# Summing Up's seven products inside PSUM, with ScalarE copying running sums, in a GFNet plus MLP-Mixer kernel

## The chip, the cores and the metric

One core of one Trainium2 chip. The metric is device time in microseconds of one execution; lower is better. A core has TensorE (matrix products into PSUM banks), VectorE and ScalarE (element-wise work, both read PSUM), GpSimd and SyncE (here mostly DMA issue and some sums).

## The reference

All fp32; batch 8, sequence 3008, width 256.

```python
X = np.fft.rfft(x, axis=1)                    # x: (8, 3008, 256)
y = np.fft.irfft(X * (filt_r + 1j * filt_i), n=3008, axis=1)
h = np.maximum(y.transpose(0, 2, 1) @ w_tok1, 0) @ w_tok2     # 3008 -> 256 -> 3008
u = y + h.transpose(0, 2, 1)
out = u + np.maximum(u @ w_ch1, 0) @ w_ch2    # 256 -> 1536 -> 256
```

## The kernel before

The transforms are products with DFT tables in two factors (47 x 64). A first stretch transforms batch 0 and rounds and combines the fp32 weights. From there the loop `mix` runs: for 8 batches, 6 tiles of the sequence (`m`, 512 columns, the last 448), 6 blocks of the hidden width (`jp`), one iteration each, 288 in all. Beside them the generator `dft` works off the next batch's transform in pieces; `mix` yields at marked places of an iteration (0, 1, 1.5, 2) and the outer loop decides there whether a piece is emitted. Instructions of an engine stand in the order in which this Python emits them (`manual_schedule`); nothing reorders them.

Both channel products, Up (256 to 1536, then ReLU) and Down (1536 to 256), are done block by block with a seven-product scheme (Strassen-Winograd) on 2x2 blocks. A product is one `matmul` call of 128x128 weights with 256 columns (224 in the last tile), and the chip executes it as two passes, each with its own weight load.

For Up, the right-hand sums `v` (4 x 256 columns) are made once a tile by `u_sums`, and the sums over the seven products give the four blocks of `hh`: `up_first` (L977) computes products 0, 5, 6 and 4 into the four halves of two PSUM banks (`pg`, two buffers), and ScalarE copies product 0 to SBUF (L980, tile `s`). `up_middle` has VectorE add product 5 to it, and then that to products 6 and 4. `up_last` (L993) computes products 1, 2 and 3 into banks that have been read, VectorE makes the four blocks by two sums of 512 columns, and ScalarE applies the ReLU to each pair of blocks (L998). All VectorE sums go through `v`, so they show as L955.

Down lags by one iteration. `h_sums` make the four sums `t` of the previous iteration's `hh` on VectorE (one of 512 columns, two of 256), and `down` (L1011) multiplies `hh` and `t` into four banks `po`, which accumulate over the six `jp`. When a tile's last block has passed, `finish` adds the banks to `u`: ScalarE copies one part (L1071), VectorE does the rest in steps (`a`, `b_`, `c`, `d`, two transposes), taken from a list two at a time by `one_step`; two of them right at the end of the iteration. The output leaves through GpSimd's queue (L1019).

The next tile's `u` is computed by `u_part` at fixed places (`own`, `new`); its products stand at L898. The token product of the next batch (L841, ended by VectorE's `c` sums and ScalarE's L858) stands in each batch's 33rd iteration. The transform's spectral products are VectorE's L709, two of 1024 columns, followed by L714 and L715; their results are copied by ScalarE (L692). ScalarE's other transform copies are L544.

One iteration emits, in this order: `up_first` and `up_middle`; `h_sums`; Down part 0 (three products); a part of the next `u`; a place for transform work; `up_last`; steps of `finish`; Down part 1 (two products); a place; Down part 2 (two products); `finish` when a tile is complete; a place.

Of the kernel before, what the change touches and what calls it, by code (L numbers as in the profile page):

```python
# [10 lines left out]
FP32 = mybir.dt.float32  # L11
I64 = mybir.dt.int64
U32 = mybir.dt.uint32
AF = mybir.ActivationFunctionType
# [9 lines left out]
P = 128  # L24
# [104 lines left out]
def kernel(  # L129
# [11 lines left out]
    nc = tc.nc  # L141
# [34 lines left out]
    tp = pool("tp", 2)  # L176
    vp = pool("vp", 2)
    sp = pool("sp", 1)
# [4 lines left out]
    def bank(tag):  # L183
        return (psg if tag == "pg" else psum).tile([P, 512], FP32, tag=tag, name="ps_" + tag)
# [30 lines left out]
    chan = []  # L215
# [653 lines left out]
    def width(m):  # L869
        return 512 if m < MT - 1 else 448  # L870
# [83 lines left out]
    def v(out, in0, in1, op=ALU.add):  # L954
        nc.vector.tensor_tensor(out=out, in0=in0, in1=in1, op=op)  # L955
# [12 lines left out]
    def h_sums(hh, t, w):  # L968

        h = hh[:, :, 0:w // 2]  # L970
        return sums(t[:, :, 0:w // 2], h[:, 1:3], h[:, 0:2], h[:, 0], h[:, 3])

    def up_first(jp, ut, vt, w, g):
        hw = w // 2
        for ps, n, mov in ((g[0][:, 0], 0, ut[:, 0, 0:hw]), (g[0][:, 1], 5, vt[:, 2, 0:hw]),
                           (g[1][:, 0], 6, vt[:, 0, 0:hw]), (g[1][:, 1], 4, vt[:, 1, 0:hw])):
            nc.tensor.matmul(ps[:, 0:hw], chan[0][:, jp, n, :], mov, start=True, stop=True)  # L977

        s = sp.tile([P, 3, 256], FP32, tag="s", name="s")[:, :, 0:hw]
        nc.scalar.copy(out=s[:, 0], in_=g[0][:, 0, 0:hw])  # L980
        return s

    def up_middle(hh, w, g, s):
        hw = w // 2
        u2 = hh[:, 2, 0:hw]
        v(u2, g[0][:, 1, 0:hw], s[:, 0])
        v(s[:, 1:3], g[1][:, :, 0:hw], u2.unsqueeze(1).to_broadcast([P, 2, hw]))

    def up_last(jp, ut, vt, w, g, s, hh):
        hw = w // 2  # L990
        for ps, n, mov in ((g[0][:, 0], 1, ut[:, 1, 0:hw]), (g[0][:, 1], 2, ut[:, 1, hw:w]),
                           (g[1][:, 1], 3, vt[:, 3, 0:hw])):
            nc.tensor.matmul(ps[:, 0:hw], chan[0][:, jp, n, :], mov, start=True, stop=True)  # L993
        h = hh[:, :, 0:hw]
        for i, add in enumerate((s[:, 0:2], s[:, 2].unsqueeze(1).to_broadcast([P, 2, hw]))):
            hs = h[:, 2 * i:2 * i + 2]
            v(hs, g[i][:, :, 0:hw], add)
            nc.scalar.activation(out=hs, in_=hs, func=AF.Relu)  # L998

    def down(m, jp, part, hh, t, po):  # L1000
        hw = width(m) // 2
        if not po:
            for i in range(4):
                po.append(bank("po%d" % i).rearrange("p (s n) -> p s n", s=2))
        b11, b21, b22 = (hh[:, i, 0:hw] for i in (0, 3, 2))
        t1, t3, t2, t4_ = (t[:, i, 0:hw] for i in range(4))

        todo = (((0, 0, 1, 0, 1, b21), (0, 1, 0, 1, 2, b22), (2, 0, 1, 0, 0, b11)),
                ((1, 1, 1, 0, 6, t1), (3, 0, 1, 1, 4, t3)), ((2, 1, 0, 1, 5, t2), (1, 0, 0, 1, 3, t4_)))
        for i, j, first, last, n, mov in todo[part]:  # L1010
            nc.tensor.matmul(po[i][:, j, 0:hw], chan[1][:, jp, n, :], mov, start=(jp == 0 and first == 1),  # L1011
                             stop=(jp == JP - 1 and last == 1))
# [89 lines left out]
    h1s, uts, vts = {}, {}, {}  # L1102
# [22 lines left out]
    def mix(next_ready):  # L1125

        wait = []
        pos, hhs, tts = {}, {}, {}

        def loads(b):  # L1130
            if b + 1 < B and next_ready(b):
                for c in wait:
                    t4_load(b + 1, c)
                wait.clear()


        own = ({(3, 0): (0,), (3, 2): (1,)}, {(2, 2): (0,), (3, 0): (1,), (3, 2): (2, 3)})
        new = {(JP - 2, 0): (0, 1), (JP - 1, 0): (2, 3)}

        def u_parts(b, m, jp, place):  # L1140
            parts = own[b > 0] if m + 1 < MT else new if b + 1 < B else {}
            now = parts.get((jp, place), ())
            b, m = (b, m + 1) if m + 1 < MT else (b + 1, 0)
            for part in now:
                u_part(b, m, part)
            if now and now[-1] == max(p for ps in parts.values() for p in ps):
                if m:
                    wait.append(m)
                todo_v.extend(v_steps(b, m))
                if b and (b, m) < (B - 1, MT - 2):  # L1150
                    w2m_load((m + 2) % MT)

        to_dram = [f for m in range(MT) for f in w2_sums(m)]
        w1_todo, w1_out = w1_sums()
        items = [(b, m, jp) for b in range(B) for m in range(MT) for jp in range(JP)]
        n = MT * JP
        for i in range(len(items) + 1):
            now, old = i < len(items), i >= 1
            if not now:
                bo, mo, jo = items[i - 1]  # L1160
                t = tp.tile([P, 4, 256], FP32, tag="t", name="t")
                last_item(bo, mo, jo, hhs.pop(i - 1), t, uts[bo, mo], pos[bo, mo])
                break
            if JP - 2 <= i < JP + 2:
                for _ in range(6 if i > JP - 2 else 1):
                    if w1_todo:
                        w1_todo.pop(0)()
            elif i >= 2 * JP and i % 2 and w1_out:
                w1_out.pop(0)()
            if i and ended[0] < len(tiles):  # L1170
                convert_middle()
                convert_end(False)
                convert_middle()
            if now:
                b, m, jp = items[i]
                if i % n == 0:
                    wait.append(0)
                w = width(m)
                hhs[i] = hp.tile([P, 4, 256], FP32, tag="hh", name="hh")
                g = [bank("pg").rearrange("p (s n) -> p s n", s=2) for _ in range(2)]  # L1180
                s = up_first(jp, uts[b, m], vts[b, m], w, g)
                up_middle(hhs[i], w, g, s)
            while todo_h1:
                todo_h1.pop()()
            if i < JP:
                one_step()
            if old:
                bo, mo, jo = items[i - 1]
                tts[i - 1] = tp.tile([P, 4, 256], FP32, tag="t", name="t")
                for f in h_sums(hhs[i - 1], tts[i - 1], width(mo)):  # L1190
                    f()
                down(mo, jo, 0, hhs[i - 1], tts[i - 1], pos.setdefault((bo, mo), []))
            if now:
                u_parts(b, m, jp, 0)
            copies()
            yield b, i % n, 0
            if ended[0] < len(tiles):
                if i == 0:
                    convert_middle()
                convert_end(False)  # L1200
            if now:
                up_last(jp, uts[b, m], vts[b, m], w, g, s, hhs[i])
                if b + 1 < B and i % n == n - 4:
                    t4_sums(b + 1, 0)
            one_step()
            if i >= JP:
                one_step()
            if now and b + 1 < B:
                if n - 4 - W1S <= i % n < n - 4:
                    w1_load(i % n - (n - 4 - W1S))  # L1210
                if i % n == n - 4:
                    t4_sums(b + 1, 1)
            copies()
            loads(b)
            yield b, i % n, 1
            if old:
                down(mo, jo, 1, hhs[i - 1], tts[i - 1], pos[bo, mo])
            yield b, i % n, 1.5
            if old:
                down(mo, jo, 2, hhs.pop(i - 1), tts.pop(i - 1), pos[bo, mo])  # L1220
                if jo == JP - 1:
                    todo_v.extend(finish(bo, mo, uts[bo, mo], pos[bo, mo]))
                    one_step()
                    one_step()
            if now:
                if b + 1 < B and i % n == n - 4:
                    h1s[b + 1] = yield from token_product(b + 1)
                u_parts(b, m, jp, 2)
                if jp == JP - 1:
                    while todo_v and m + 1 == MT:  # L1230
                        one_step()
                if i >= 8 and to_dram:
                    to_dram.pop(0)()
                if i in (28, 29):
                    w2m_load(i - 28)
            loads(b)
            yield b, i % n, 2
        while todo_v:
            one_step()

    with tc.manual_schedule():
# [69 lines left out]
        n = MT * JP  # L1311
# [58 lines left out]
```

## Time and profile before

| | |
|---|---|
| time, median of 3 runs (lowest to highest) | 2405.31 us (2405.25 to 2406.09) |
| span of the profiled execution | 2403.2 us |
| what lies around the span, against the median | 2.1 us |
| TensorE busy | 2359.4 us, 98% |
| VectorE busy | 1951.0 us, 81% |
| ScalarE busy | 689.8 us, 29% |
| GpSimd busy | 638.3 us, 27% |
| granted TensorE clock, mean | 0.995 |
| the mixing loop begins | at about 140 us |

The profiled execution has no time of its own beside its span; the runs were timed without a profile. In the profile PE is a matmul pass on TensorE, PEld its weight load, DVE VectorE, ACT ScalarE, POOL GpSimd. Matmul passes overlap, so that a PE that is busy throughout can still have a little room; where it matters, the distance from one pass's start to the next tells more than the busy share.

### The profile page before, as it was taken

The numbers are of one execution on the slowest core, as the hardware profiler recorded it, in microseconds if no ns is written. First come the engines' busy times: TensorE is split into PE (matmuls) and PEld (weight loads), VectorE is DVE, ScalarE is ACT, GpSimd is POOL, SyncE is SP. The second block draws the span as 40 slices with busy tenths as digits, with TensorE's granted clock in tenths as the row PEclk, the third lists the DMA queues.
The fourth block names the chain that finished last, engine by engine and source line by source line (L and its number), as shares of the span: only waits on it lengthen the run. The fifth ranks groups of instructions, "written<-read, shape, count | busy, mean of one in ns | idle before, by whom it ended". The sixth has DMA issues, their size and how long they took to land.

```text
span 2403.2 us, 37053 instructions
## 1 busy us (share of the span) xinstructions
PE 2359.4 (98%) x13132; PEld 2012.9 (84%) x13132; DVE 1951.0 (81%) x3669; ACT 689.8 (29%) x1339; POOL 638.3 (27%) x1124
## 2 busy tenths in 40 slices
PE   7989999999999999999999999999999999999998
PEld 4667888888898888988888888988889888898887
DVE  7798887788887888788887788778887788877786
ACT  5732222222223222232222222222222322212222
POOL 7477434211211121112112311221121112112121
PEclk8999999999999999999999999999999999999999
DMA  9963546333353333533344333533335433331100
GB/s 218 241 195 121 152 119 226 114 118 85 106 188 124 100 95 117 189 118 96 98 145 158 117 93 103 186 120 107 90 114 172 132 98 98 108 130 32 39 14 21
DMA packets 189719, 294.28 MB, mean 122 GB/s; under 512 B 34444, under 2 KB 124962, under 8 KB 189534
## 3 DMA queue, kind: packets, MB, share of 16 engines
q1 hardware_dynamic: 148046, 231.24, 31.0%
q0 software_dynamic: 34688, 53.83, 8.6%
q10 hardware_dynamic: 6800, 6.85, 0.9%
q8 instruction: 104, 1.70, 0.3%
q14 instruction: 81, 0.66, 0.1%
HBM read 209.06 MB, written 82.72 MB: 121 GB/s over the span
## 4 chain that ended last, share of the span: by engine, by line
PE 92%; DVE 3%; DMA 2%; issue 1%; POOL 1%; ACT 1%; SPq 0%; ACTq 0%; DVEq 0%; POOLq 0%
PE ps_po L1011 35%; PE ps_pg L977 20%; PE ps_pg L993 15%; PE ps_b L528 3%; PE ps_b L841 3%; PE ps_acc L898 3%; PE ps_acc L841 2%; PE ps_pg L528 2%; PE ps_b L898 2%; PE ps_b L876 2%; PE ps_acc L876 2%; DVE both L284 0%; DVE t L955 0%; DMA g_tmp<-t 0%; DVE both L289 0%
## 5 line engine op out<-in xcount | busy, mean ns | idle before, releaser
L1019 POOL DMA_DIRECT2D out_dram<-r x752 | 408.3, 550 | 1452.0 <-issue 1028.0
L998 ACT ACTIVATE hh<-hh 128x512 f32<-128x512 f32 (+1 forms) x576 | 348.0, 621 | 1017.7 <-DVE hh L955 1013.8
L955 DVE TENSOR_TENSOR hh<-ps_pg,s 128x512 f32<-128x512 f32 (+3 forms) x864 | 482.5, 586 | 171.3 <-ACT s L980 161.1
L1011 PE MATMUL ps_po<-t,wc 128*128 128x256 f32 (+1 forms) x2296 | 558.1, 380 | 0.7 <-DVE t L955 0.7
L1011 PEld LDWEIGHTS ps_po<-t,wc 128*128 128x128 f32 x2296 | 427.7, 190 | 95.6 <-issue 38.7
L977 PE MATMUL ps_pg<-v,wc 128*128 128x256 f32 (+1 forms) x1728 | 412.6, 375 | 1.4 <-POOL wc L386 1.4
L1011 PE MATMUL ps_po<-hh,wc 128*128 128x256 f32 (+1 forms) x1722 | 411.5, 375 | 0.6 <-POOL wc L387 0.6
L977 PEld LDWEIGHTS ps_pg<-v,wc 128*128 128x128 f32 x1728 | 327.9, 190 | 39.6 <-POOL wc L386 2.2
L1011 PEld LDWEIGHTS ps_po<-hh,wc 128*128 128x128 f32 x1722 | 326.8, 190 | 38.4 <-POOL wc L387 1.4
L993 PE MATMUL ps_pg<-u,wc 128*128 128x256 f32 (+1 forms) x1152 | 292.3, 376 | 5.7 <-DVE hh L955 5.6
L955 DVE TENSOR_TENSOR t<-t,hh 128x256 f32<-128x256 f32 (+1 forms) x576 | 247.1, 429 | 19.8
L993 PEld LDWEIGHTS ps_pg<-u,wc 128*128 128x128 f32 x1152 | 217.2, 190 | 37.1 <-DVE hh L955 10.8
L955 DVE TENSOR_TENSOR s<-ps_pg,hh 128x512 f32<-128x512 f32 (+1 forms) x288 | 196.1, 681 | 30.0
L980 ACT COPY s<-ps_pg 128x256 f32<-128x256 f32 (+1 forms) x288 | 105.8, 368 | 332.4 <-PE ps_pg L977 329.1
L955 DVE TENSOR_TENSOR t<-hh 128x512 f32<-128x512 f32 (+1 forms) x288 | 194.4, 675 | 0.6 <-ACT hh L998 0.6
L977 PE MATMUL ps_pg<-u,wc 128*128 128x256 f32 (+1 forms) x576 | 169.3, 376 | 3.9 <-DVE hh L955 3.9
L993 PE MATMUL ps_pg<-v,wc 128*128 128x256 f32 (+1 forms) x576 | 169.2, 375 | 0.0
L977 PEld LDWEIGHTS ps_pg<-u,wc 128*128 128x128 f32 x576 | 108.1, 190 | 19.7 <-DVE hh L955 7.5
L993 PEld LDWEIGHTS ps_pg<-v,wc 128*128 128x128 f32 x576 | 109.2, 190 | 13.0
L955 DVE TENSOR_TENSOR u<-ps_acc,u 128x256 f32<-128x256 f32 (+1 forms) x84 | 46.2, 550 | 72.4 <-PE ps_acc L898 50.1
L955 DVE TENSOR_TENSOR u<-ps_b,u 128x512 f32<-128x512 f32 (+2 forms) x126 | 74.5, 591 | 28.8 <-PE ps_b L898 26.7
L898 PE MATMUL ps_acc<-w 128*128 128x256 f32 (+1 forms) x336 | 85.2, 376 | 0.0
(164 smaller groups left out, 2686.8 us busy)
## 6 DMA issues: line engine op xcount, KB each, us to landing
w<-w_tmp SPq DMA_DIRECT2D x84, 448.0 KB
w<-w_tmp SPq DMA_DIRECT2D x35, 896.0 KB
out_dram<-r POOLq DMA_DIRECT2D x696, 32.0 KB, 3.4
g_tmp<-t SPq DMA_DIRECT2D x112, 192.0 KB
t<-g_tmp SPq DMA_DIRECT2D x42, 512.0 KB
t<-z_tmp SPq DMA_DIRECT2D x196, 96.0 KB
z_tmp<-t SPq DMA_DIRECT2D x72, 256.0 KB
wb<-wbi_t SPq DMA_DIRECT2D x56, 256.0 KB
```

The lines of the kernel that those rows point to most:

```text
L528: nc.tensor.matmul(outs(i, j), stat(i, j), mov(i, j), start=True, stop=True)
L841: nc.tensor.matmul(ps[:, at], w[:, n], mov, start=(j == 0 and i in (0, 2)), stop=(j == AP - 1 and i >= 5))
L876: nc.tensor.matmul(ps[:, ds(q * P, n)], t4[b, c][:, r, ts(dh, P)], wai[:, 0:n], start=(first and q == 0), stop=(not first and q == 3))
L898: nc.tensor.matmul(ps[:, ds(j * hw, hw)], h1[:, n, :], w2m[m % 2][:, at, 0:hw], start=(i < 2 and j == 0), stop=(j == len(todo) - 1))
L955: nc.vector.tensor_tensor(out=out, in0=in0, in1=in1, op=op)
L977: nc.tensor.matmul(ps[:, 0:hw], chan[0][:, jp, n, :], mov, start=True, stop=True)
L980: nc.scalar.copy(out=s[:, 0], in_=g[0][:, 0, 0:hw])
L993: nc.tensor.matmul(ps[:, 0:hw], chan[0][:, jp, n, :], mov, start=True, stop=True)
L998: nc.scalar.activation(out=hs, in_=hs, func=AF.Relu)
L1011: nc.tensor.matmul(po[i][:, j, 0:hw], chan[1][:, jp, n, :], mov, start=(jp == 0 and first == 1), stop=(jp == JP - 1 and last == 1))
L1019: q.dma_start(bass.AP(tensor=ob.tensor, offset=ob.offset + row * D + g * cw, ap=[[N1 * D, 32], [D if h else -D, n], [1, cw]]), blocks[ts(g ...
```

## The change

Up's sums move into the accumulation of the banks. In one bank a half, `x`, takes products 0, 5, 6 and 2 one on top of the other, and ScalarE copies the running sum out after each (into `hh` blocks 0, 3 and 2; the last one goes through the ReLU straight into block 1). In the other bank, half `z` holds product 1, and half `y` product 4 and later 3 on top of it. VectorE adds `z` to block 0, the earlier `y` to block 2 and the later `y` to block 3, and ScalarE applies the ReLU to each block on its own. `h_sums` of the previous iteration come ahead of Up's sums, and Down is cut into four parts that stand between Up's steps.

```diff
-    def up_first(jp, ut, vt, w, g):
...
-        for ps, n, mov in ((g[0][:, 0], 0, ut[:, 0, 0:hw]), (g[0][:, 1], 5, vt[:, 2, 0:hw]),
-                           (g[1][:, 0], 6, vt[:, 0, 0:hw]), (g[1][:, 1], 4, vt[:, 1, 0:hw])):
-            nc.tensor.matmul(ps[:, 0:hw], chan[0][:, jp, n, :], mov, start=True, stop=True)
-
-        s = sp.tile([P, 3, 256], FP32, tag="s", name="s")[:, :, 0:hw]
-        nc.scalar.copy(out=s[:, 0], in_=g[0][:, 0, 0:hw])
-        return s
-
-    def up_middle(hh, w, g, s):
...
-    def up_last(jp, ut, vt, w, g, s, hh):
...
+    def up_steps(jp, ut, vt, w, hh):
+        hw = w // 2
+        one, two = (bank("pg").rearrange("p (s n) -> p s n", s=2)[:, :, 0:hw] for _ in range(2))
         h = hh[:, :, 0:hw]
+
+        def times(out, n, mov, start=False):
+            nc.tensor.matmul(out, chan[0][:, jp, n, :], mov, start=start, stop=True, skip_group_check=True)
+
+        def joined(i, ps):
+            v(h[:, i], ps, h[:, i])
+            nc.scalar.activation(out=h[:, i], in_=h[:, i], func=AF.Relu)
+
+        x, y, z = one[:, 0], two[:, 0], two[:, 1]
+        times(x, 0, ut[:, 0, 0:hw], start=True)
+        nc.scalar.copy(out=h[:, 0], in_=x)
+        times(z, 1, ut[:, 1, 0:hw], start=True)
+        times(y, 4, vt[:, 1, 0:hw])
+        times(x, 5, vt[:, 2, 0:hw])
+        nc.scalar.copy(out=h[:, 3], in_=x)
+        joined(0, z)
+        yield
+        times(x, 6, vt[:, 0, 0:hw])
+        nc.scalar.copy(out=h[:, 2], in_=x)
+        joined(2, y)
+        yield
+        times(x, 2, ut[:, 1, hw:w])
+        nc.scalar.activation(out=h[:, 1], in_=x, func=AF.Relu)
+        times(y, 3, vt[:, 3, 0:hw])
+        joined(3, y)
+        yield
...
-        todo = (((0, 0, 1, 0, 1, b21), (0, 1, 0, 1, 2, b22), (2, 0, 1, 0, 0, b11)),
-                ((1, 1, 1, 0, 6, t1), (3, 0, 1, 1, 4, t3)), ((2, 1, 0, 1, 5, t2), (1, 0, 0, 1, 3, t4_)))
+        todo = (((2, 0, 1, 0, 0, b11), (0, 1, 1, 0, 2, b22)), ((0, 0, 0, 1, 1, b21), (1, 1, 1, 0, 6, t1)),
+                ((3, 0, 1, 1, 4, t3),), ((2, 1, 0, 1, 5, t2), (1, 0, 0, 1, 3, t4_)))
...
-                g = [bank("pg").rearrange("p (s n) -> p s n", s=2) for _ in range(2)]
-                s = up_first(jp, uts[b, m], vts[b, m], w, g)
-                up_middle(hhs[i], w, g, s)
+                ups = up_steps(jp, uts[b, m], vts[b, m], w, hhs[i])
+            if old:
+                bo, mo, jo = items[i - 1]
+                tts[i - 1] = tp.tile([P, 4, 256], FP32, tag="t", name="t")
+                for f in h_sums(hhs[i - 1], tts[i - 1], width(mo)):
+                    f()
+            if now:
+                next(ups)
             while todo_h1:
                 todo_h1.pop()()
             if i < JP:
                 one_step()
             if old:
-                bo, mo, jo = items[i - 1]
-                tts[i - 1] = tp.tile([P, 4, 256], FP32, tag="t", name="t")
-                for f in h_sums(hhs[i - 1], tts[i - 1], width(mo)):
-                    f()
                 down(mo, jo, 0, hhs[i - 1], tts[i - 1], pos.setdefault((bo, mo), []))
+            if now:
+                next(ups)
+            if old:
+                down(mo, jo, 1, hhs[i - 1], tts[i - 1], pos[bo, mo])
             if now:
                 u_parts(b, m, jp, 0)
             copies()
...
             if now:
-                up_last(jp, uts[b, m], vts[b, m], w, g, s, hhs[i])
+                next(ups)
...
             yield b, i % n, 1
             if old:
-                down(mo, jo, 1, hhs[i - 1], tts[i - 1], pos[bo, mo])
+                down(mo, jo, 2, hhs[i - 1], tts[i - 1], pos[bo, mo])
             yield b, i % n, 1.5
             if old:
-                down(mo, jo, 2, hhs.pop(i - 1), tts.pop(i - 1), pos[bo, mo])
+                down(mo, jo, 3, hhs.pop(i - 1), tts.pop(i - 1), pos[bo, mo])
```

More of the change, by code (lines that the diff above doesn't have):

```diff
@@ L983, in up_middle @@
-    def up_middle(hh, w, g, s):
[L984 to L987, printed above, removed]
-    def up_last(jp, ut, vt, w, g, s, hh):
[L990 to L993, printed above, removed]
-        h = hh[:, :, 0:hw]
[L995 to L998, printed above, removed]
+        one, two = (bank("pg").rearrange("p (s n) -> p s n", s=2)[:, :, 0:hw] for _ in range(2))
```

## The prediction

> **What bounds the kernel now.** I read the page first, then stretches, waits, groups by form, and last the timeline of single iterations of the mixing loop. Page and a 200 us stretch:
>
> ```profile
> PE 2359.4 (98%) x13132; PEld 2012.9 (84%) x13132; DVE 1951.0 (81%) x3669; ACT 689.8 (29%) x1339; POOL 638.3 (27%) x1124
> ...
> PE 92%; DVE 3%; DMA 2%; issue 1%; POOL 1%; ACT 1%; SPq 0%; ACTq 0%; DVEq 0%; POOLq 0%
> ```
>
> ```profile
> 1100.00:1300.00 200.00, 200.00 (x1208) 175.80 (x1210) 166.18 (x317) 51.50 (x104) 37.84 (x69) 1.00 0.42 127
> ```
>
> PE is never idle there, at clock 1.00, and owns 92% of the ending chain. VectorE's 81% is off the path: relieving it buys nothing unless PE waits for it. The waits say how little PE does:
>
> ```profile
> PE ps_pg L993 <- DVE hh L955: 5.6, 4, 3.2
> PE ps_pg L977 <- DVE hh L955: 3.9, 4, 2.1
> ```
>
> The prices, by form (busy, mean ns):
>
> ```profile
> L998 ACT ACTIVATE hh<-hh 128x512 f32<-128x512 f32 x480 | 294.8, 630 | 861.0 <-DVE hh L955 857.1 <-DMA z_tmp<-t 3.9
> L955 DVE TENSOR_TENSOR hh<-ps_pg,s 128x256 f32<-128x256 f32 x240 | 101.4, 422 | 137.9 <-ACT s L980 137.8
> L980 ACT COPY s<-ps_pg 128x256 f32<-128x256 f32 x240 | 89.3, 372 | 304.7 <-PE ps_pg L977 301.5 <-DMA z_tmp<-t 1.9 <-ACT t L544 1.2
> ```
>
> Timeline of an iteration after a tile's end, and of the next one's start (start, length):
>
> ```profile
> 1203.10 0.59 PE L977 MATMUL ps_pg<-u,wc 128*128 128x256 f32 x2
> 1203.53 1.46 PE L977 MATMUL ps_pg<-v,wc 128*128 128x256 f32 x6
> 1204.22 0.37 ACT L980 COPY s<-ps_pg 128x256 f32<-128x256 f32 x1 [0.78 <-PE ps_pg L977]
> 1204.75 0.41 DVE L955 TENSOR_TENSOR r<-ps_po,r 128x256 f32<-128x256 f32 x1
> 1205.60 0.69 DVE L955 TENSOR_TENSOR s<-ps_pg,hh 128x512 f32<-128x512 f32 x1
> 1206.21 0.68 DVE L955 TENSOR_TENSOR t<-hh 128x512 f32<-128x512 f32 x1
> 1206.92 0.89 DVE L955 TENSOR_TENSOR t<-t,hh 128x256 f32<-128x256 f32 x2
> ...
> 1211.23 0.59 PE L977 MATMUL ps_pg<-u,wc 128*128 128x256 f32 x2
> ...
> 1211.57 1.21 DVE L709 TENSOR_TENSOR p<-ps_acc,filt 128x1024 f32<-128x1024 f32 x1
> ```
>
> A product is two matmul passes. Six take 1.46 us, one lasts 0.38, so a pass starts every 0.216 and a product every 0.432. From an iteration's first pass, the last operation of `finish` queued ahead ends at 1204.75+0.41-1203.10 = 2.06; the spectral product (L709) ends at 1.55. Today that is harmless.
>
> **What goes and comes.** Per iteration VectorE loses one 256-column sum (0.42) and three 512-column ones (0.69), 2.49 us, for three of 256, 1.27 us: 1.2 us x 288 = 350 us off VectorE, all off the path. `h_sums` move ahead of Up's sums on VectorE, three instructions without a DMA; Down's products are regrouped from 3, 2, 2 to 2, 2, 1, 2. ScalarE goes from one copy and two 512-column ReLUs (1.63 us) to three copies and four ReLUs of 256 (about 0.42 each: 512 and 448 columns take 630 and 577 ns, so 0.83 ns a column), 2.8 us of a 6.04 us iteration. PE keeps 14 products: nothing gained in steady state. DMA issues keep number and places; they shift with what they follow.
>
> What is new is a chain through one half bank, called x here: product 0, copied out; product 5 on top, copied; 6, copied; 2, through a ReLU. Each addition waits for the copy before. The other bank holds z (product 1) and y (4, then 3 on top after VectorE has read it). In units from the iteration's start, in its new order, the products start at: 0 at 0; 1, 4 next; 5 at 1.30; two of Down; 6 at 2.59; two of Down; 2 at 3.89; 3 at 4.32; three of Down; 6.04.
>
> **Undisturbed iteration.** Product 0's passes end at 0.22+0.38 = 0.60; ScalarE starts 0.09 later (1204.22 against 1203.10+3x0.216+0.38); copy 0.37, end 1.06. The return to PE is in another row:
>
> ```profile
> 455.54 0.41 DVE L955 TENSOR_TENSOR hh<-ps_pg,s 128x256 f32<-128x256 f32 x1
> 456.01 0.73 PEld L993 LDWEIGHTS ps_pg<-u,wc 128*128 128x128 f32 x4 [0.42 <-DVE hh L955]
> 456.01 0.92 PE L993 MATMUL ps_pg<-u,wc 128*128 128x256 f32 x3
> ```
>
> Weights load 0.05 after the releaser ends, and three passes take 0.92 instead of 0.81: 0.10 for the restart. So 1.06+0.15 = 1.21 against 1.30: hidden with 0.08 to spare. The same holds for 6 and 2, each again six passes behind its predecessor. Product 3 waits for VectorE's sum into y, which follows the third copy: 3.65+0.04+0.42+0.15 = 4.26 against 4.32, hidden too. Both ends of this cost: nothing, or if a handover takes 0.1 more than these rows, about 0.1 on four waits of some 230 uncovered iterations, 92 us. I take nothing, since every term is a row's; the other end goes to a rival. The banks come back in time too: where the spectral products had both (L692), their second copy ends 0.21 after product 0's start and product 1 may go at 0.36, before its slot at 0.43.
>
> **Where the cover is gone.** ScalarE takes its list in order: copy, copy, ReLU of z's sum, third copy. That ReLU waits for VectorE's sum into z, which now stands behind the three sums for Down (`h_sums`), which stand behind whatever VectorE has left from the iteration before. Behind the waiting ReLU stand the third copy, the other ReLUs and `finish`'s or the transform's copies; for the third copy wait VectorE's sum into y and product 2, and behind that all of PE. Let VectorE be free of old work at E after the iteration's start. `h_sums` end 1.52 later (1207.81 after 1206.29); z's sum, overlapping 0.08, ends E+1.86; ReLU from E+1.89 to E+2.31; copy, overlapping 0.03, to E+2.65; plus 0.15: product 2 starts at E+2.80, not 3.89; the wait is E-1.08, and product 3 adds 0.03. So each iteration with E above 1.05, without other matmuls ahead of product 2, loses **E-1.05**. In 448-column tiles the slot is 3.40 and the chain 2.59: E-0.81. Before, the first sums came ahead of `h_sums` and no copy stood behind a ReLU that they free.
>
> I read E of every iteration off VectorE's rows:
> - After a tile's end, 512 columns: E = 2.06, less 0.16 because ScalarE's copy for `finish`, today held to 6.03 by the 512-column ReLUs, can start at 5.87. 29 x 0.85 = 24.7; ten others with more queued (E 1.97 to 3.02, mostly 2.65) 13.1. Together 37.8 us.
> - The same in 448 columns: 8 x 1.2 = 9.7 us.
> - Behind an L709 pair: 56. E = 1.55 in 32 (0.50 each), 1.61 in 13 (0.56), 2.17 in 6 (1.12), five more 5.0: 35.0 us. These are tied to PE, so VectorE's relief does not move them.
> - After the token product: 7, E = 1.55, and ScalarE there gets two 0.41 copies (L858) behind a sum ahead of the third copy: 1.4 x 7 = 9.8 us.
> - A handful of others, 1.7 us.
>
> Sum 94. Against it: in the weight-conversion stretch (140 to 184 us) VectorE is the bound; it loses 1.2 us an iteration but waits 0.83 for the third copy (ReLU 0.42 + copy 0.37 + handovers), so about 1 us gained over three iterations; the tail gains 1 us by narrower last sums and ReLU. Net +92.
>
> The profiled span is 2403.2 us, the median 2405.31; 2.1 lie outside and stay. 2405.3+92 = **2497 us**.
>
> **Two rules against the rows.** PE's idle of 3.22 us before 220.25 is followed by a stretch at granted clock 0.57:
>
> ```profile
> 220.20:224.20 4.00, 3.95 (x11) 3.18 (x11) 3.83 (x7) 1.05 (x2) 0.00 (x0) 0.57 0.58 162
> ```
>
> Idles of about 1 us in the three iterations before 184 us leave passes 0.216 apart. My new waits are 0.5 to 1.6, so I add nothing for the clock. The Trainium skill ("TensorE: Matmul & The Clock Gate", "A second HAM failure mode") says that frequent micro-idles while cycling PSUM banks make the clock oscillate; by it, estimating one 3.4 us half-rate window for each of 110 waits, some 187 us more, 2684. No row here shows such an effect of short idles. The same skill ("Perfetto Trace Analysis", "Matmuls") wants groups rotated through banks so that evacuation overlaps; this change serialises one bank, and by the rows above that alone is hidden.
>
> **Rivals.**
> - Faster: the ScalarE chain is covered everywhere, and VectorE's relief ends today's PE waits. For it: the waits above and 34 us of idle PE in the first 220 us (25.6 before 150, 8.5 after). Against it: before 140 us the mixer hasn't begun; from there to 245 us iterations exceed their passes' 0.216 each by some 12 us that VectorE could end. It gives 2393 to 2400. It decides if z's sum ends by 2.85 in nearly all iterations, which E = 1.90 contradicts.
> - No change: VectorE's relief pulls E below 1.05 nearly everywhere, and the start refunds the rest: within 5 us. Against it: L709's E is set by PE.
> - Much slower: undisturbed handovers miss as well, 0.1 on four waits: 2497+92 = 2589.
> - That the change does less than it says: three of VectorE's sums stay; counted above.
>
> **How the numbers follow.** Forecast 0.80, much slower 0.10, faster 0.07, no change 0.03. The forecast's own range: 0.2 us either way on 110 waits is 22 us, and half of my E's shortened by VectorE's relief another 20: 2455 to 2535. Taking a start on the far case gives 2455 to 2545. Slower by over 0.2% (about 5 us, what a measurement of this kernel can tell) 0.90, within 0.03, faster 0.07.
>
> **What would show it.** Right: PE waits for ScalarE at the x-accumulations, about one iteration in three, 0.5 to 1.4 us each, after `finish` and after L709; plain iterations stay 6.04; VectorE about 350 us less busy; clock 1.00. Wrong: plain iterations longer than 6.04 (handovers mis-sized), no waits after `finish` (order mis-read), or a lower granted clock.

## The result, and the profile after

The changed kernel takes 2483.22 us (median; 2482.67 to 2484.33) against 2405.28 us before: 1.0329 times as long, interval 1.0316 to 1.0341, 78 us. The profiled span is 2482.0 us, 78.8 more. The page, busy times and the chain that ended last:

```profile
PE 2386.9 (96%) x13132; PEld 1989.7 (80%) x13132; DVE 1649.1 (66%) x3381; ACT 978.6 (39%) x2491; POOL 638.1 (26%) x1124
...
PE 71%; DVE 18%; ACT 5%; issue 4%; DMA 1%; POOL 0%; DVEq 0%; ACTq 0%; SPq 0%; POOLq 0%
```

VectorE is 302 us less busy, as intended, and yet it has entered the chain: 18% of the chain that ended last now runs through VectorE, where it was 3%. PE does the same 13132 passes and has gaps. In a 200 us stretch (busy time of PE, PEld, DVE, ACT, POOL, then the granted clock):

```profile
1100.00:1300.00 200.00, 195.57 (x1108) 162.24 (x1107) 135.99 (x270) 79.18 (x207) 34.67 (x64) 1.00 0.37 109
```

PE was never idle in this stretch before; now it is for 4.4 us, at the same clock of 1.00. The counts of passes, 1108 here and 1208 before, can't be set against each other: the changed kernel is behind by then, and its stretch begins 26 iterations and has no token product, where the stretch before had 25 and the token product's 168 passes (L841). The 26 iterations are together 8.0 us longer than the same ones before. Who is waited for (total us, times, longest):

```profile
ACT hh L983 <- DVE hh L955: 523.9, 811, 3.4
...
PEld ps_pg L979 <- ACT hh L995: 99.1, 114, 2.5
...
PE ps_pg L979 <- ACT hh L995: 54.5, 112, 2.0
```

L995 is the third copy of x, L983 the ReLUs behind VectorE's sums: 114 weight loads wait for that copy, in 288 iterations. PE itself stands 112 times, 0.49 us on the mean. One of them, an iteration after a tile's end that starts at 1147.27 (timeline; start, length):

```profile
1147.27 1.03 PE L979 MATMUL ps_pg<-u,wc 128*128 128x256 f32 x4
...
1148.71 0.42 DVE L955 TENSOR_TENSOR r<-ps_po,r 128x256 f32<-128x256 f32 x1
...
1149.05 0.68 DVE L955 TENSOR_TENSOR t<-hh 128x512 f32<-128x512 f32 x1
...
1149.76 0.88 DVE L955 TENSOR_TENSOR t<-t,hh 128x256 f32<-128x256 f32 x2
1149.86 0.59 PE L979 MATMUL ps_pg<-v,wc 128*128 128x256 f32 x2
...
1150.57 0.42 DVE L955 TENSOR_TENSOR hh<-ps_pg,hh 128x256 f32<-128x256 f32 x1
...
1151.02 0.42 ACT L983 ACTIVATE hh<-hh 128x256 f32<-128x256 f32 x1 [1.45 <-DVE hh L955]
1151.34 0.35 ACT L995 COPY hh<-ps_pg 128x256 f32<-128x256 f32 x1
1151.72 0.42 DVE L955 TENSOR_TENSOR hh<-ps_pg,hh 128x256 f32<-128x256 f32 x1 [0.74 <-ACT hh L995]
1151.74 0.30 PEld L979 LDWEIGHTS ps_pg<-u,wc 128*128 128x128 f32 x2 [0.83 <-ACT hh L995]
```

From top to bottom it is one chain: the last step of `finish` (ends 1149.13), the three `h_sums`, z's sum, its ReLU, the third copy, product 2's weights. ScalarE stood idle 1.45 us in front of the ReLU, with a copy behind it whose data, product 6's sum, was there at 1150.45 (the passes from 1149.86), 0.9 us before the copy began. Set against the same iterations before, 153 of 288 are as long as they were within 0.05 us and 119 are longer by more than 0.2 us.

### The profile page after: what moved, and what is told of

It is laid out like the page before. It is cut to its first block, busy times and chain, and to the rows that moved or that the text cites. A ratio compares the mean times of both kernels' runs of the same rounds, so it can differ in the third digit from the quotient of the medians.

```text
span 2482.0 us, 37697 instructions
## 1 busy us (share of the span) xinstructions
PE 2386.9 (96%) x13132; PEld 1989.7 (80%) x13132; DVE 1649.1 (66%) x3381; ACT 978.6 (39%) x2491; POOL 638.1 (26%) x1124
## 4 chain that ended last, share of the span: by engine, by line
PE 71%; DVE 18%; ACT 5%; issue 4%; DMA 1%; POOL 0%; DVEq 0%; ACTq 0%; SPq 0%; POOLq 0%
PE ps_pg L979 26%; PE ps_po L1015 23%; DVE p L709 5%; DVE t L955 5%; PE ps_b L528 3%; PE ps_b L841 3%; PE ps_acc L898 3%; DVE u L955 2%; DVE hh L955 2%; PE ps_acc L841 2%; ACT hh L983 2%; PE ps_b L898 2%; PE ps_pg L528 2%; PE ps_acc L876 2%; PE ps_b L876 2%
## 5 line engine op out<-in xcount | busy, mean ns | idle before, releaser
L955 DVE TENSOR_TENSOR hh<-ps_pg,hh 128x256 f32<-128x256 f32 (+1 forms) x864 | 360.0, 417 | 501.9 <-ACT hh L995 264.5
L979 PE MATMUL ps_pg<-v,wc 128*128 128x256 f32 (+1 forms) x2304 | 633.7, 377 | 4.0 <-ACT hh L987 3.2
L1015 PE MATMUL ps_po<-t,wc 128*128 128x256 f32 (+1 forms) x2296 | 603.6, 379 | 0.6 <-DVE t L955 0.5
L983 ACT ACTIVATE hh<-hh 128x256 f32<-128x256 f32 (+1 forms) x864 | 356.2, 412 | 524.0 <-DVE hh L955 523.9
L979 PEld LDWEIGHTS ps_pg<-v,wc 128*128 128x128 f32 x2304 | 424.0, 190 | 73.0 <-DVE hh L955 15.8
L1015 PE MATMUL ps_po<-hh,wc 128*128 128x256 f32 (+1 forms) x1722 | 458.5, 375 | 0.0
L1015 PEld LDWEIGHTS ps_po<-hh,wc 128*128 128x128 f32 x1722 | 326.9, 190 | 37.8 <-POOL wc L387 0.8
L955 DVE TENSOR_TENSOR t<-t,hh 128x256 f32<-128x256 f32 (+1 forms) x576 | 247.5, 430 | 33.8 <-ACT hh L991 0.5
L991 ACT COPY hh<-ps_pg 128x256 f32<-128x256 f32 (+1 forms) x288 | 105.9, 368 | 259.0 <-PE ps_pg L979 259.0
L987 ACT COPY hh<-ps_pg 128x256 f32<-128x256 f32 (+1 forms) x288 | 105.9, 368 | 258.8 <-PE ps_pg L979 255.5
L955 DVE TENSOR_TENSOR t<-hh 128x512 f32<-128x512 f32 (+1 forms) x288 | 196.2, 681 | 2.4 <-ACT hh L999 2.4
L999 ACT ACTIVATE hh<-ps_pg 128x256 f32<-128x256 f32 (+1 forms) x288 | 107.2, 372 | 61.4 <-PE ps_pg L979 58.3
L995 ACT COPY hh<-ps_pg 128x256 f32<-128x256 f32 (+1 forms) x288 | 103.1, 358 | 32.0 <-PE ps_pg L979 30.9
L955 DVE TENSOR_TENSOR u<-ps_b,u 128x512 f32<-128x512 f32 (+2 forms) x126 | 74.8, 593 | 59.4 <-PE ps_b L898 57.2
L955 DVE TENSOR_TENSOR u<-ps_acc,u 128x256 f32<-128x256 f32 (+1 forms) x84 | 46.2, 550 | 93.7 <-PE ps_acc L898 61.3
L709 DVE TENSOR_TENSOR p<-ps_b,filt 128x1024 f32<-128x1024 f32 x56 | 68.5, 1223 | 26.8 <-PE ps_pg L528 21.6
L692 ACT COPY t<-ps_pg 128x512 f32<-128x512 f32 x98 | 52.6, 589 | 70.6 <-PE ps_pg L528 70.6
```

Source lines behind the costliest of these rows:

```text
L709: nc.vector.tensor_tensor(out=prods[c, h], in0=pss[h].unsqueeze(1).to_broadcast([P, 2, 2, D]), in1=filts[c % FB], op=ALU.mult)
L979: nc.tensor.matmul(out, chan[0][:, jp, n, :], mov, start=start, stop=True, skip_group_check=True)
L983: nc.scalar.activation(out=h[:, i], in_=h[:, i], func=AF.Relu)
L987: nc.scalar.copy(out=h[:, 0], in_=x)
L991: nc.scalar.copy(out=h[:, 3], in_=x)
L999: nc.scalar.activation(out=h[:, 1], in_=x, func=AF.Relu)
```

## Experiments

The theory: the third copy of x is held by the ReLU ahead of it in ScalarE's list, and that ReLU by VectorE's order. Rival A: the round trip through one bank (copy, then restart) is itself the cost. Rival B: short waits lower TensorE's clock. Rival C: ScalarE's longer list is the cost.

**One ScalarE instruction moved.**

```diff
-        joined(0, z)
+        v(h[:, 0], z, h[:, 0])
         yield
         times(x, 6, vt[:, 0, 0:hw])
         nc.scalar.copy(out=h[:, 2], in_=x)
+        nc.scalar.activation(out=h[:, 0], in_=h[:, 0], func=AF.Relu)
```

> The changed kernel with one ScalarE instruction moved: the ReLU of block 0 (z's sum) stands behind the third copy of x instead of ahead of it. My theory (the third copy is held by that ReLU, which waits for VectorE's sum into z, which stands behind h_sums and old work): product 2 no longer waits, product 3 only where VectorE is free later than 1.96 us, so nearly all of the 78 us go; the iteration after the token product keeps some 10 us, because ScalarE's two copies of 0.41 us still stand ahead of the third copy: 2405+10+5, 2410 to 2425. Rival A (the round trip through the one bank x is the cost, copy and restart each time): nothing changes, 2475 to 2490. Rival B (short PE waits lower the granted clock): time and clock as in the changed kernel.

Measured 2417.38 us, ratio to before 1.0054 (1.0039 to 1.0069). Weight loads that wait for the third copy (now L995 too):

```profile
PEld ps_pg L979 <- ACT hh L995: 10.9, 7, 1.8
```

Of 114 waits seven are left, one in each of the first seven batches, in the iteration after the token product; these seven iterations are together 10.7 us longer than before the change. 66 of the 78 us went with one instruction's place; work, banks and the number of ScalarE instructions are the changed kernel's. Rivals A and C fall. So does rival B for the changed kernel: its mean granted clock is 0.995, that of the kernel before.

**VectorE's order alone.** `h_sums` behind `next(ups)`:

```diff
+            if now:
+                next(ups)
+            if old:
                 for f in h_sums(hhs[i - 1], tts[i - 1], width(mo)):
                     f()
-            if now:
-                next(ups)
```

> The changed kernel with h_sums behind VectorE's sum into z instead of ahead of it; ScalarE's order is the changed kernel's. My theory: the sum into z ends by 2.3 us even after a tile's end, the ReLU and the third copy keep their slots, and what is left is the sum into y behind h_sums (it decides only where VectorE is free later than about 2 us) and the 10 us after the token product: 2410 to 2427. Rival A (round trip through bank x): 2475 to 2490. Rival C (it is ScalarE's list alone, its seven instructions an iteration in place of three): ScalarE's work is the same here, so 2475 to 2490.

Measured 2417.99 us, 1.0051 (1.0034 to 1.0067). The same list of waits:

```profile
PEld ps_pg L979 <- ACT hh L995: 10.4, 7, 1.5
```

The chain can be cut at either link. The early weight-conversion stretch did worse here (iterations 0 to 8 together 1.1 us longer than in the kernel before, and 1.6 us shorter in the first experiment), the rest alike.

**The order without the accumulation.** The kernel before, with `h_sums` ahead of `up_middle`:

```diff
+            if old:
+                ...
+                for f in h_sums(hhs[i - 1], tts[i - 1], width(mo)):
+                    f()
+            if now:
+                up_middle(hhs[i], w, g, s)
-                up_middle(hhs[i], w, g, s)
...
-                for f in h_sums(hhs[i - 1], tts[i - 1], width(mo)):
-                    f()
```

> The kernel before with one thing of the change alone: h_sums stand ahead of up_middle on VectorE. No accumulation in PSUM, no added copy. My theory (the order is the cause): the first pass of up_last then waits for the first sum, at 3.02 us of an iteration against VectorE free + 1.86 + 0.15, so an iteration loses VectorE free - 1.0, over some 115 iterations: 2405+95, 2485 to 2515. Rival A (accumulation through one bank is the cost): 2400 to 2412. Rival B (clock): as rival A, there being no more short waits than before.

Measured 2489.96 us, 1.0351 (1.0336 to 1.0366): 7 us slower than the change, with no product accumulated and no copy added.

```profile
PEld ps_pg L993 <- DVE hh L955: 116.4, 116, 3.7
```

116 waits, here for the first sum itself and not for a copy behind it. So the order on VectorE costs as much by itself, and what costs in the change is not that Up is summed in PSUM but the order that came with it.

**How much slack an undisturbed iteration has.**

```diff
-        todo = (((2, 0, 1, 0, 0, b11), (0, 1, 1, 0, 2, b22)), ((0, 0, 0, 1, 1, b21), (1, 1, 1, 0, 6, t1)),
+        todo = (((2, 0, 1, 0, 0, b11),), ((0, 1, 1, 0, 2, b22), (0, 0, 0, 1, 1, b21), (1, 1, 1, 0, 6, t1)),
```

> The changed kernel with one Down product moved from between products 5 and 6 to between 6 and 2, so that the second copy has 0.43 us less cover. It measures the slack of an undisturbed iteration. In the changed kernel's trace the second copy ends at 2.30 and could let product 6 go at 2.46, its slot is 2.59; here the slot is 2.16, so 0.30 are lost in each iteration that doesn't already wait longer at product 2 (about 170), none in the others: 2483+51, 2520 to 2545, and 6.04 us iterations become 6.34. A rival that puts the slack at a whole product or more: 2483, within 5. A rival by which undisturbed iterations already stand at their limit (no slack): 0.43 each, 2483+73 = 2556.

Measured 2534.89 us, 1.0539 (1.0523 to 1.0555). All 288 iterations now wait at product 6, and those that were 6.04 us long are 6.34:

```profile
PEld ps_pg L979 <- ACT hh L991: 123.5, 288, 0.9
PEld ps_pg L979 <- ACT hh L995: 64.7, 112, 2.6
```

166 iterations are 0.30 us longer than in the changed kernel, and 109, which already waited at product 2, are as long as there. 0.43 us of cover removed cost 0.30: the slack was 0.13 us. That is the limit within which rival A is wrong; with one Down product fewer in the gap it would be right.

**VectorE busy 0.6 us longer.** The first of `h_sums` done twice:

```diff
-                for f in h_sums(hhs[i - 1], tts[i - 1], width(mo)):
+                hs = h_sums(hhs[i - 1], tts[i - 1], width(mo))
+                for f in (hs[0],) + hs:
                     f()
```

> The changed kernel with the first of the three h_sums (512 columns, 0.60 us from start to start) computed twice, the second time into the same place: VectorE's old work ends 0.60 later in every iteration, PE and ScalarE have the same work. My theory: about 115 iterations that wait today wait 0.60 longer (+69), and the 40 or so after the transform's third or fourth step, where VectorE is free at 0.89 and nothing covers, begin to wait by about 0.35 (+14): 2483+83, 2555 to 2575. A rival by which VectorE, 66% busy, has room for 0.6 us in 6 us: 2483, within 5. A rival by which the waits come from the copies' round trip: 2483 too.

Measured 2614.16 us, 1.0864 (1.0847 to 1.0881): 131 us over the changed kernel, more than expected (2555 to 2575).

```profile
PEld ps_pg L979 <- ACT hh L995: 217.3, 202, 2.9
```

The two sums start 0.72 us apart and not 0.60 (probably because both write the same place; that was not tried); in most of the iterations that already waited the loss grew by that 0.72, one for one. And 202 weight loads wait instead of 114: iterations where VectorE had been free at 0.89 lose 0.55, and even the ones at 0.53, which I had not counted, lose 0.19. An engine at 66% had no room for 0.7 us in 6. In the profiled run some 9 us are something else: in six iterations TensorE's clock fell to half after these waits (last section).

**All links cut.** The late ReLU; VectorE's order z's sum, first `h_sums`, y's sum, the other two; the token product's last sum and copies behind the third copy:

```diff
...
-                for f in h_sums(hhs[i - 1], tts[i - 1], width(mo)):
-                    f()
+                hs = h_sums(hhs[i - 1], tts[i - 1], width(mo))
             if now:
                 next(ups)
-            while todo_h1:
-                todo_h1.pop()()
+            if old:
+                hs[0]()
...
             if now:
                 next(ups)
+            while todo_h1:
+                todo_h1.pop()()
             if old:
+                hs[1]()
+                hs[2]()
                 down(mo, jo, 1, hhs[i - 1], tts[i - 1], pos[bo, mo])
```

> The changed kernel with the ReLU of z's sum behind the third copy, VectorE's order z's sum, first h_sum, y's sum, other two h_sums, and the end of the token product (VectorE's sum and ScalarE's two copies) behind the third copy. My theory: nothing stands ahead of the third copy but two copies and PE; y's sum is late only where VectorE is free later than about 2.5; the 10 us after the token product go: from the 2417 of the first step alone to 2403 to 2408, as long as the kernel before, because PE is the bound again; the weight-conversion stretch may move it by 3 either way. Rival A (round trip through one bank): 2475 to 2490. A rival by which 0.3 of cover are too little for the chain anyway: 2415 to 2420, as the first step alone.

Measured 2402.09 us against 2405.49 us in the same runs: 0.9988 (0.9979 to 0.9997), faster than the kernel before by a margin close to what can be measured, and just below the 2403 to 2408 expected. The same stretch as above:

```profile
1100.00:1300.00 200.00, 199.73 (x1208) 174.49 (x1207) 138.59 (x293) 78.00 (x204) 37.67 (x69) 1.00 0.42 129
```

1208 passes, as before the change, and here for the same work (25 iterations and one token product in each), with VectorE at 69% instead of 83%. Iteration by iteration the middle of the run is as long as in the kernel before; of the 3.3 us by which the span is shorter, the loop begins 0.9 us earlier, its first nine iterations take 1.4 us less, and the rest is spread. The loop's start lies between 138.6 and 141.4 us in the eight profiles, though no edit is ahead of it, so that part need not be the change's. At most the rest is what VectorE's relief was worth.

## Why the prediction was right

The mechanism was right: 2497 us were forecast with 2455 to 2545, the slowdown came from product 2 waiting for the third copy, undisturbed iterations stayed at 6.04, and the clock at 1.00. Its classes, with iterations compared one by one between the two traces:

| iterations | predicted us | measured us |
|---|---|---|
| 39 after a tile's end, 512 columns | 37.8 | 31.2 |
| 8 after a tile's end, 448 columns | 9.7 | 9.0 |
| 56 behind an L709 pair | 35.0 | 25.3 |
| 7 after the token product | 9.8 | 10.6 |
| all others, and the loop's start | 1.7, less 1 for the weight conversion and 1 for the tail | 2.6 |

The terms that were mis-sized:
- The common wait after a tile's end was 0.72, not 0.85. VectorE was free at 1.86 instead of 1.90; the third copy takes 0.35 and overlaps the ReLU by 0.09, where I had 0.37 and 0.03.
- Six of the tile ends with more queued cost 0.94, where E of 2.65 and E-1.05 make 1.60. E was right (2.65 in the changed kernel) and PE did stand for about 1.5 at product 2, but the same iteration before already lost some 0.5 us to waits of its own.
- "These are tied to PE, so VectorE's relief does not move them" was wrong for six of the L709 pairs. There VectorE, not PE, was late before; it is now free at 1.64 instead of 2.17, and the loss is 0.58, not 1.12. The other pairs cost 0.48 and 0.54 against 0.50 and 0.56.
- Iteration 8, in that class, was 3.4 us shorter, where every one of the class was forecast longer. Before, PE stood 3.22 us there and then ran at half clock; now it stands 2.05 us one iteration earlier and slows there, so the two iterations together lose 0.7 less.
- ScalarE starts 0.035 us after a product's last pass ends, not 0.09. That is why undisturbed iterations had 0.13 us of slack, not 0.08: wrong on the safe side.
- Not foreseen: 0.34 us in the iteration after the token product's next (six times), where the part of the next `u` stands later in PE's list and its bank comes free late for the transform (`PE ps_b L528 <- DVE u L955: 1.6, 6, 0.3` among the changed kernel's waits, and not among those before).
- The weight conversion gave nothing back: the four iterations that begin before 184 us are together 1.2 us longer, where 1 us was to be gained.
- VectorE is 302 us less busy, not 350: `h_sums` and the other sums take as long as before, but my 2.49 us of removed sums counted full lengths, which overlap their neighbours by 0.08.
- The range's upper ends do not come out of its own terms: 2497 plus 22 is 2519, and 2535 and 2545 have no sum behind them. The lower end, 2455, has, and the miss of 14 us lies on that side.

Of the Trainium skill, "TensorE: Matmul & The Clock Gate" ("A second HAM failure mode") would have added half-rate windows for the short waits, 2684 us by the estimate in the prediction. The changed kernel does not bear that out: 112 waits of 0.49 us on the mean, 2.0 at most, left the mean granted clock at 0.995, as before. But the prediction's ground for it, that idles of about 1 us are harmless, does not hold throughout: in the fifth experiment waits of 0.50 and 1.20 us were followed by half clock five times out of six. "Perfetto Trace Analysis" ("Matmuls") asks that independent groups rotate through banks, so that the copying out of one overlaps the next. The changed kernel keeps one sum in one bank and lets Down's products cover the copies: that costs nothing as long as 0.13 us of slack remain, and 0.30 us an iteration with one product fewer in a gap (fourth experiment).

The rival that it would get faster failed where it was expected to, at z's sum. With the order mended it comes true by 3 us, which is less than its 5 to 12. Why not more was not tried; with the order mended, PE still waits for ScalarE's first copy of x (4.9 us in five waits) and for VectorE's sums `t` (3.0 us in two).

## What to carry to other kernels

Work taken off an engine that nobody waits for bought at most 3 us in 2405 here, but the handovers that come with it can put that engine on the path: look at where the new wait stands in each engine's list and at what is queued ahead of it, not at busy shares. In-order lists pass a delay on: a ready copy behind a ReLU that waits for VectorE is as late as VectorE is. For a chain with slack of a tenth of a microsecond, put first in every list what the bound engine will wait for, and let results that are needed an iteration later come behind it.

## What the runs showed of the hardware that was not expected

In the changed kernel an idle time of TensorE of 2.05 us was followed by half speed. In its early part passes stand 0.43 us apart for over 2 us after it; the stretch's granted clock:

```profile
212.00:217.00 5.00, 3.86 (x22) 2.46 (x22) 2.62 (x6) 1.89 (x5) 4.77 (x5) 0.66 0.40 123
```

Another idle time of 2.11 us, before the second iteration of the kernel before, was followed by passes at 0.32 and then 0.22 us, so length alone does not decide it.

Nor does it take 2 us. In the fifth experiment the iterations 37, 73, 109, 145, 181 and 217 (counted from 0) each hold the same two waits of PE, 0.50 and 1.20 us. In iteration 37:

```profile
483.03 0.67 PE L1015 MATMUL ps_po<-t,wc 128*128 128x256 f32 x2 [0.50 <-DVE t L955]
...
484.90 0.93 PE L979 MATMUL ps_pg<-u,wc 128*128 128x256 f32 x2 [1.20 <-ACT hh L995]
```

In all of them but 145 the clock then was at half for 3.4 us, and these five are 12.0 us long where 145 is 10.35. The stretch behind the second wait in 37, and the same place in 145:

```profile
485.23:488.64 3.41, 3.41 (x14) 1.83 (x16) 2.00 (x6) 1.22 (x3) 0.00 (x0) 0.50 0.02 5
1426.48:1429.89 3.41, 3.41 (x24) 1.51 (x23) 2.58 (x7) 1.30 (x4) 0.00 (x0) 1.00 0.00 0
```

The same waits thus cost 1.6 us more or nothing more, in one execution. A sixth such stretch follows a single wait of 1.80 us, in iteration 105; the waits of 1.80 to 1.86 us at the same place of six other batches have none behind them. What decides it was not tried.
